# Attention scores by 64-row matmuls for all head pairs, masks by 64-row ones too, second buffers in the room of the kq tiles, and a new planned order

## The chip, the cores and the metric

The kernel runs on one core of one Trainium2 chip. A core has a TensorE (PE, matmuls, with its weight loads shown apart as PEld), a VectorE (DVE), a ScalarE (ACT), a GpSimd (POOL) and a SyncE (SP), whose queue here issues every DMA. The metric is the device time in microseconds (us) of one execution, and its median over several. A profile shows the span from the first to the last instruction, and the device time is a little longer than that.

## The reference, cut to what matters

Eight batches with eight heads of 576 tokens and 64 channels go through softmax attention with a block-causal mask (blocks of 64 tokens), and the result, 4608 tokens of 512 channels, through a feed-forward layer with 2048 hidden units and a rational activation.

```
scores = scale * np.matmul(q, k.transpose(0, 1, 3, 2))
mask = block_i >= block_j                      # blocks of 64 tokens
scores = np.where(mask, scores, -1000000000.0)
attn = softmax(scores)                         # over the last axis
x = (attn @ v), heads side by side             # 4608 x 512
h = x @ w_in
g = (a0 + a1 h + a2 h^2 + a3 h^3) / (1 + |b0||h| + |b1|h^2 + 1e-6)
out = g @ w_out
```

All of it is float32. The kernel keeps that accuracy with three products of split numbers: each operand is written as a high part in the fp32r format plus a low rest, and high*high, high*low and low*high are added.

## The kernel before, in words

**Attention.** Heads are worked in 32 pairs (`NP`), the two heads of a pair side by side in the 128 partitions. `load` fetches q, k and v of a pair. `prep` transposes q and k on TensorE (L410, three 96-row transposes into one PSUM bank), and ACT (L414) and DVE (L417) write the high and low halves into an `hl` tile: head 0 of the pair in partitions 0 to 63, head 1 in 64 to 127. `scores` works five stripes `t` of query rows, which see 64, 192, 320, 448 and 576 keys; the last stripe goes in two pieces of 288, and a piece is never narrower than 256 columns. Per piece and head come a maximum (DVE L521, L517), an exponential with its sum (ACT L525), a reciprocal and the scaling of the probabilities (POOL L532 to L545), their transposes (PE L566), a split of these into high (ACT L581) and low (DVE L583), and `pv`, the product with v (PE L604, 15 and 27 matmuls a pair), whose result is split (L617, L619) and stored to a scratch in HBM (L622). `vprep` splits v into the two `vpad` tiles (L453, L455).

**Two ways to score.** Pairs 0 and 1 (`nat`) score straight from the `hl` tiles: three matmuls with 64 rows for each head (L486), the two heads in turn, one in the upper and one in the lower half of the array, and the mask added by a small bf16 matmul with 32 rows for each head (L490). Pairs 2 to 31 score from `kq` tiles: eight DMAs a pair (L432) copy the `hl` halves so that one 128-row matmul makes high*high plus the mask (L509) and another makes the two mixed products (L510). The constant mask rows of the kq tiles are built at the start by POOL (L334 to L342) and copied by DVE (L362).

**Feed-forward.** `split_weights` splits the weights (`place`, 32 pieces: DVE L637 to L643, ACT L635, L647, L651, POOL L648, L652). In the first part of the program `ffn0` (PE L741, L760) works half of the hidden units for 256 tokens at a time between the attention work; when attention is done, its room takes the other half of the weights, and `ffn1` (PE L855, L858, L881) does the rest for 512 tokens at a time.

**The order.** Every operation is recorded with a cost, a priority and its dependences, and `Plan.order` plays a list schedule on these numbers: the order in which operations start there is the order of each engine's queue. Buffers come from `Pool`s, the eight PSUM banks from one pool with quotas (`QA` six for attention, `QH` and `QO` two each for ffn0). `gate` holds feed-forward work back until attention has come to a given pair.

The attention tiles exist once (`QR`, `VR`, `HL`, `P`, `XS`, `vpad`), the kq tiles twice:

```
    QR = tiles(att, 1, [LP, 2 * NL, D], F32, "qr")
    HL = [tiles(att, 1, [128, 2, S], F32R, f"hl{i}") for i in range(2)]
    P = [tiles(att, 1, [128, 2, NK[t]], F32, f"p{t}") for t in range(5)]
    kqt = [[att.tile([128, 4, S], F32R, name=f"kq{'ab'[i]}{'ab'[j]}") for j in range(2)] for i in range(2)]
```

Of the kernel before, what the change touches and what calls it, by code (L numbers as in the profile page):

```python
# [60 lines left out]
class Op:  # L61
    __slots__ = ("eng", "c", "d", "fn", "pri", "gives", "deps", "outs", "bufs", "n", "ready", "at", "end", "seq")


PORT = 220.0
LATENCY = {"PE": 250, "ACT": 40,
           "DVE": 40.0, "POOL": 150, "SP": 60.0, "-": 0.0}


class Plan:  # L70
# [5 lines left out]
    def op(self, eng, cd, fn, rd=(), wr=(), pri=0.0, after=(), port=False, gives=()):  # L76
        o = Op()
        o.gives = gives
        o.eng, o.c, o.d, o.fn, o.pri, o.seq = eng, cd[0] + PORT * port, cd[1] + PORT * port, fn, pri, len(self.ops)
# [14 lines left out]
        if eng in ("ACT", "DVE") and any(b.quota for b in bufs):  # L94
            o.pri -= 15
# [4 lines left out]
    def order(self):  # L100
# [14 lines left out]
        left = len(self.ops)  # L115

# [14 lines left out]
        while left:  # L131
            best = None
            for e in LATENCY:
# [4 lines left out]
                for p, s, o in sorted(able[e])[:24]:  # L138
# [93 lines left out]
def attn_ffn_kernel(  # L232
# [37 lines left out]
    X.free = []  # L270
# [30 lines left out]
    XS = tiles(att, 1, [128, 2, 320], F32R, "xs")  # L301
# [3 lines left out]
    vpad = [att.tile([128, 128 + 4 * 192], F32R, name=f"vp{x}") for x in "hl"]  # L305
# [3 lines left out]
    op("SP", (500, 100), lambda: nc.sync.dma_start(out=coef[:, 0:4], in_=ca.partition_broadcast(128)), wr=["ca"], pri=20)  # L309
    op("SP", (500, 100), lambda: nc.sync.dma_start(out=coef[:, 4:6], in_=cb.partition_broadcast(128)), wr=["cb"], pri=20)  # L310
# [14 lines left out]
    p0 = P[0].tiles[0]  # L325
# [75 lines left out]
    def prep(p, s, which):  # L401
# [18 lines left out]
        if p < NATP:  # L420
            return
# [528 lines left out]
```

## Time and profile before

| | |
|---|---|
| device time, median of 3 runs | 1282.99 us (1279.13 to 1284.53) |
| device time of the profiled execution | 1278.76 us |
| its span | 1276.6 us |
| PE busy | 1230.6 us, 96% |
| DVE, ACT, POOL busy | 942.3, 891.4, 848.5 us (74, 70, 66%) |
| DMA moved | 195.12 MB, mean 153 GB/s |
| 0 to 160 us: PE, DVE busy, mean PE clock | 133.28, 125.51 us, 0.93 |
| 160 to 800 us: the same | 628.53, 495.90 us, 1.00 |
| 800 us to the end: the same | 468.79, 320.88 us, 1.00 |

The first stage is attention with the weight split, the second attention between `ffn0`, the third `ffn1`. The ends of matmuls in the trace are modelled and overlap the next ones, so what a matmul costs is read from start to start. The granted clock has two levels, 1.0 (2.4 GHz) and 0.5 (1.2 GHz); the column of a window is their mean.

### The profile page before, as it was taken

Reading aid. Unit: us, or ns where it says so; the run is one execution under the profiler, and the core shown is the slowest. Engines: PE = TensorE matmul, PEld = TensorE weight load, DVE = VectorE, ACT = ScalarE, POOL = GpSimd, SP = SyncE. Lnnn points to the kernel's source line nnn. Section 1 sums busy time; section 2 is a strip of 40 time slices with the busy share of each in tenths; the row PEclk is TensorE's granted clock in tenths of the full one; section 3 lists DMA queues with packets and bytes.
Section 4 is the critical chain, followed back from the end, with each engine's and each line's share of the span. In section 5 each row is a group of like instructions: output and inputs, shape, how many; then the busy total and the mean of one; then the engine's idle time right before and its main releaser. Section 6 shows DMA issues by size and latency. Waiting matters only on the chain.

```text
span 1276.6 us, 23262 instructions
## 1 busy us (share of the span) xinstructions
PE 1230.6 (96%) x7560; PEld 1088.4 (85%) x7560; DVE 942.3 (74%) x1916; ACT 891.4 (70%) x2230; POOL 848.5 (66%) x1218
## 2 busy tenths in 40 slices
PE   7879999999999999999999999999999999999997
PEld 5669799899998999999988999888888888888885
DVE  7867887778787777778876876666676777677664
ACT  6778787778877788787787886555655555555554
POOL 6757876767767767676767776566665666665564
PEclk8989999999999999999999999999999999999999
DMA  5888876678777857786696741911142233224110
GB/s 147 217 235 213 221 191 174 179 191 210 192 194 185 225 162 200 180 212 187 165 236 181 196 133 63 379 47 41 59 132 67 89 109 118 81 66 132 34 33 33
DMA packets 222615, 195.12 MB, mean 153 GB/s; under 512 B 129312, under 2 KB 183584, under 8 KB 222496
## 3 DMA queue, kind: packets, MB, share of 16 engines
q1 hardware_dynamic: 222496, 193.65, 55.5%
q8 instruction: 60, 0.98, 0.3%
q14 instruction: 59, 0.48, 0.1%
HBM read 95.95 MB, written 44.56 MB: 110 GB/s over the span
## 4 chain that ended last, share of the span: by engine, by line
PE 68%; DVE 7%; DMA 7%; ACT 7%; POOL 6%; issue 3%; SPq 1%; POOLq 0%; ACTq 0%; DVEq 0%
PE psd L855 4%; PE psf L855 4%; PE psb L881 4%; PE psh L881 4%; PE pse L881 3%; PE psg L881 3%; PE psf L604 3%; DMA osa<-in_moe_w_in_dram 3%; PE psc L881 2%; PE psa L881 2%; PE psa L855 2%; PE psc L855 2%; PE psc L760 2%; PE psg L855 1%; PE psa L741 1%
## 5 line engine op out<-in xcount | busy, mean ns | idle before, releaser
L681 POOL TENSOR_SCALAR va<-ub,bab 128x512 f32<-128x512 f32 x60 | 46.8, 780 | 93.0 <-ACT ub L678 91.1
L681 POOL TENSOR_SCALAR vb<-ua,bab 128x512 f32<-128x512 f32 x57 | 44.2, 776 | 91.8 <-ACT ua L678 91.7
L703 POOL TENSOR_TENSOR glb<-sa,ghb 128x512 fp32r<-128x512 f32 x58 | 75.5, 1302 | 20.1 <-ACT ghb L702 17.7
L683 POOL TENSOR_TENSOR ub<-va,ub 128x512 f32<-128x512 f32 x60 | 77.9, 1299 | 4.6
L703 POOL TENSOR_TENSOR gla<-sb,gha 128x512 fp32r<-128x512 f32 x58 | 75.6, 1303 | 7.8 <-ACT gha L702 7.7
L455 POOL TENSOR_TENSOR vpl<-vra,vph 128x256 fp32r<-128x256 f32 (+1 forms) x128 | 67.8, 539 | 19.5 <-ACT vph L453 11.6
L683 POOL TENSOR_TENSOR ua<-vb,ua 128x512 f32<-128x512 f32 x57 | 74.0, 1298 | 4.6
L689 ACT ACTIVATE va<-ub,qcb 128x512 f32<-128x512 f32 x60 | 43.6, 727 | 46.0 <-POOL ub L683 45.8
L689 ACT ACTIVATE vb<-ua,qcb 128x512 f32<-128x512 f32 x57 | 41.3, 724 | 43.0 <-POOL ua L683 43.0
L702 ACT CAST ghb<-sa 128x512 fp32r<-128x512 f32 x58 | 36.1, 622 | 26.8 <-DVE sa L699 26.7
L702 ACT CAST gha<-sb 128x512 fp32r<-128x512 f32 x58 | 36.2, 624 | 11.1 <-DVE sb L699 10.9
L453 ACT CAST vph<-vra 128x256 fp32r<-128x256 f32 (+1 forms) x128 | 39.1, 324 | 1.8 <-POOL vph L323 0.4
L695 DVE SCALAR_TENSOR_TENSOR ub<-ub,psf 128x512 f32<-128x512 f32 x23 | 15.8, 686 | 25.5 <-ACT psf L693 25.4
L695 DVE SCALAR_TENSOR_TENSOR ub<-ub,psd 128x512 f32<-128x512 f32 x21 | 14.4, 687 | 26.5 <-ACT psd L693 26.3
L741 PE MATMUL psa<-x,wiha 128*128 128x256 f32 x176 | 33.2, 288 | 0.5 <-DVE sb L699 0.4
L741 PE MATMUL psf<-x,wiha 128*128 128x256 f32 x176 | 32.8, 285 | 0.5 <-DMA x<-xscr 0.5
L678 ACT ACTIVATE ua<-psf 128x512 f32<-128x512 f32 x25 | 15.0, 598 | 25.3 <-PE psf L855 21.1
L678 ACT ACTIVATE ua<-psd 128x512 f32<-128x512 f32 x24 | 14.3, 598 | 21.7 <-PE psd L855 19.4
L703 POOL TENSOR_TENSOR glb<-sb,ghb 128x512 fp32r<-128x512 f32 x14 | 18.1, 1296 | 16.1 <-ACT ghb L702 16.1
L741 PEld LDWEIGHTS psa<-x,wiha 128*128 128x128 f32 x176 | 27.3, 191 | 1.1 <-DVE sb L699 0.6
L741 PEld LDWEIGHTS psf<-x,wiha 128*128 128x128 f32 x176 | 27.5, 191 | 0.7 <-DMA x<-xscr 0.7
L741 PE MATMUL psb<-x,wiha 128*128 128x256 f32 x144 | 27.0, 286 | 0.0
(1662 smaller groups left out, 5599.0 us busy)
## 6 DMA issues: line engine op xcount, KB each, us to landing
xscr<-xsa SPq DMA_DIRECT2D x32, 320.0 KB, 2.9
x<-xscr SPq DMA_DIRECT2D x40, 256.0 KB, 4.5
qra<-in_q_dram SPq DMA_DIRECT2D x64, 144.0 KB, 3.7
qra<-in_k_dram SPq DMA_DIRECT2D x60, 144.0 KB, 2.9
vra<-in_v_dram SPq DMA_DIRECT2D x64, 128.0 KB, 2.5
xscr<-xsa SPq DMA_DIRECT2D x32, 256.0 KB, 3.7
ppa<-pscr SPq DMA_DIRECT2D x15, 512.0 KB, 4.0
osa<-in_moe_w_in_dram SPq DMA_DIRECT2D x10, 512.0 KB, 5.2
```

Source lines behind the costliest of these rows:

```text
L453: aop("ACT", (0.833 * n + 110, 0.833 * n + 200), lambda vh=vh, src=src: nc.scalar.copy(out=vh, in_=src()), rd=rd, wr=[("v", i, 0)], pri=pr ...
L455: aop("POOL", pool(n, True), lambda vh=vh, vl=vl, src=src: nc.gpsimd.tensor_tensor(out=vl, in0=src(), in1=vh.bitcast(F32), op=ALU.subtract ...
L604: nc.tensor.matmul(bank.t[:, s0:w], lhsT=vblock(vv, x), rhs=pp, start=(x == 0 and i == 0), stop=(x == nb - 1 and i == 2))
L681: op("POOL", pool(512, False, 2), lambda: nc.gpsimd.tensor_scalar(out=vt.t, in0=ut.t, scalar1=b1, scalar2=b0, op0=ALU.mult, op1=ALU.add), ...
L683: op("POOL", pool(512, True), lambda: nc.gpsimd.tensor_tensor(out=ut.t, in0=vt.t, in1=ut.t, op=ALU.mult), rd=[vt], wr=[ut], pri=pri)
L689: op("ACT", act(512, False, 1), lambda: nc.scalar.activation(out=vt.t, in_=ut.t, func=AF.Ln, bias=qcb), rd=[ut, "qcb"], wr=[vt], pri=pri)
L695: op("DVE", dve(512), lambda: nc.vector.scalar_tensor_tensor(out=ut.t, in0=ut.t, scalar=QC, in1=r0.t, op0=ALU.add, op1=ALU.mult), rd=rk, w ...
L702: op("ACT", act(512, False), lambda: nc.scalar.copy(out=gh.t, in_=st.t), rd=[st], wr=[gh], pri=pri)
L703: op("POOL", pool(512, True), lambda: nc.gpsimd.tensor_tensor(out=gl.t, in0=st.t, in1=gh.t.bitcast(F32), op=ALU.subtract), rd=[st, gh], wr ...
L741: nc.tensor.matmul(h.t[:, j * CT:(j + 1) * CT], lhsT=w[:, dc, fs], rhs=xb[dc // 2].t[:, dc % 2, hl, :], start=(dc == 0 and i == 0), stop=( ...
L855: nc.tensor.matmul(h.t, lhsT=w[:, dc, fs], rhs=x.t[:, dc, hl, :], start=(dc == 0 and i == 0), stop=(dc == 3 and i == 2))
L881: nc.tensor.matmul(o[m].t, lhsT=g.t[:, c0:c0 + 128], rhs=w[:, ff, :], start=(a and i == 0 and j == 0), stop=(z and i == 2))
```

## The change

All 32 pairs score as pairs 0 and 1 did: six 64-row matmuls a piece, two heads in turn. The mask tiles `mq` and `mk` get a copy in the lower half and 64 rows, so the mask matmuls are 64-row too, one in each half of the array. The kq tiles, their DMAs and the large mask go. In their room stand second buffers of `QR`, `VR`, both `HL`, `P[3]`, `P[4]`, `XS` and the `vpad` pair; pair 1 no longer borrows the room of `x`. The planner's costs change: it knows 93 ns for a change of the array's mode, new costs for matmuls and POOL; priorities and the gate change (`ffn0` may run 8 instead of 12 units ahead of attention, and begins at 70 instead of 60), `pv` falls behind the next pair's scores. Where the plan shows a gap on PE before a fresh bank in its first 160 us, up to 16 transposes of the identity are put into that bank ahead of its first use.

```
+MODE = 93.0
+WARM_UNTIL, WARM_SHARE, WARM_MOST = 160e3, 0.7, 16
...
+            if e == "PE" and o.rt != rt:
+                rt = o.rt
+                o.c += MODE
+                o.d += MODE
...
-    QR = tiles(att, 1, [LP, 2 * NL, D], F32, "qr")
+    QR = tiles(att, 2, [LP, 2 * NL, D], F32, "qr")
+    VR = tiles(att, 2, [128, 9, D], F32, "vr")
+    HL = [tiles(att, 2, [128, 2, S], F32R, f"hl{i}") for i in range(2)]
+    P = [tiles(att, (1, 1, 1, 2, 2)[t], [128, 2, NK[t]], F32, f"p{t}") for t in range(5)]
...
-    kqt = [[att.tile([128, 4, S], F32R, name=f"kq{'ab'[i]}{'ab'[j]}") for j in range(2)] for i in range(2)]
...
+    mq = cpool.tile([128, 128], BF16, name="mq")
+    mk = cpool.tile([128, 64], BF16, name="mk")
...
+            def sc(i=i, c0=c0, w=w, ww=ww):
+                for a, (x, y) in enumerate(((0, 0), (0, 1), (1, 0))):
+                    for j in range(2):
+                        r = slice(64 * j, 64 * j + 64)
+                        nc.tensor.matmul(bks2[j][i].t[:, :ww], lhsT=qt.t[r, x, qs], rhs=kt.t[r, y, c0:c0 + ww],
+                                         start=(a == 0), stop=(a == 2))
+                    if a == 0 and t and c0 + w == n:
                         for j in range(2):
                             r = slice(64 * j, 64 * j + 64)
+                            nc.tensor.matmul(bks2[j][i].t[:, w - 64:w], lhsT=mq[r], rhs=mk[r], start=False, stop=False)
...
-    E0, E1 = 60, 340
+    E0, E1 = 70, 345
...
     for o in todo:
+        if o.eng == "PE" and o.fresh and o.at < WARM_UNTIL:
+            for _ in range(min(int(o.gap * WARM_SHARE / 109), WARM_MOST)):
+                nc.tensor.transpose(o.fresh.t[:, :128], ident, ident)
         o.fn()
```

Between attention and `ffn0` on PE, in the kernel before: the rows of two heads' scores from the kq tiles (`kqaa`, `kqab`; L509 and L510) stand between the product with v (L604) and the second feed-forward matmuls (L760).

```order
L604 MATMUL psa<-pt2h,vpl 128x256
L509 MATMUL psh<-kqab 128x320
L510 MATMUL psh<-kqab 128x320
L509 MATMUL psg<-kqaa 128x448
L510 MATMUL psg<-kqaa 128x448
L760 MATMUL psc<-woha,gla 128x512
```

The same kind of place now, with the 64-row score matmuls (L448, from the tiles `hl1a` and `hl0a`), the mask (L453) and the first feed-forward matmuls (L690):

```order
L515 MATMUL psc<-ident,p4b 128x128 x3
L448 MATMUL pse<-hl1a,hl0a 128x256
L448 MATMUL psd<-hl1a,hl0a 128x256
L453 LDWEIGHTS mq
L453 MATMUL pse<-mk,mq 128x64
L453 LDWEIGHTS mq
L453 MATMUL psd<-mk,mq 128x64
L448 MATMUL pse<-hl1a,hl0a 128x256
L448 MATMUL psd<-hl1a,hl0a 128x256
L448 MATMUL pse<-hl1a,hl0a 128x256
L448 MATMUL psd<-hl1a,hl0a 128x256
L690 MATMUL psb<-x,wiha 128x256 x2
```

Two heads are now always scored together, and before and behind each such run of 64-row rows stands a 128-row row. In the whole program there are 147 runs, so 294 changes between 64 and 128 rows (78 of them up to the last L553 of pair 7), where the kernel before has 14.

At the head of PE's queue before, transposes of the raw q and k (`qra`, `osa`) and then the first scores:

```order
L410 MATMUL psa<-ident,qra 128x96 x3
L410 MATMUL psb<-ident,qra 128x96 x3
L410 MATMUL psc<-ident,osa 128x96 x3
L410 MATMUL psd<-ident,osa 128x96 x3
L486 MATMUL pse<-hl1a,hl0a 128x256
```

Now, with the transposes of the identity (L869):

```order
L869 MATMUL psa<-ident 128x128 x16
L395 MATMUL psa<-ident,qra 128x96 x3
L395 MATMUL psb<-ident,qra 128x96 x3
L869 MATMUL psc<-ident 128x128 x5
L395 MATMUL psc<-ident,osa 128x96 x3
L395 MATMUL psd<-ident,osa 128x96 x3
L869 MATMUL psf<-ident 128x128 x9
L448 MATMUL pse<-hl1a,hl0a 128x256
```

There are 181 of them in all, each in a bank that no real product has filled yet, and all before the 1,340th of some 8,300 matmuls.

In SP's queue before, a stretch with the copies into the kq tiles (L432), the load of k (L389, into the one tile `qra`) and a piece of weights (L633):

```order
L389 DMA qra<-in_q_dram 96x6x64 x2
L633 DMA osa<-in_moe_w_in_dram 128x2x512
L633 DMA osb<-in_moe_w_in_dram 128x2x512
L389 DMA qra<-in_k_dram 96x6x64 x2
L432 DMA kqaa<-hl0a 64x2x576
L432 DMA kqab<-hl0a 64x2x576
L432 DMA kqaa<-hl0a 64x576
L432 DMA kqab<-hl0a 64x576
L633 DMA osa<-in_moe_w_out_dram 128x1024
```

Now, with two raw tiles (`qra`, `qrb`) and no copies:

```order
L374 DMA qra<-in_q_dram 96x6x64 x2
L582 DMA osb<-in_moe_w_in_dram 128x2x512
L374 DMA qrb<-in_k_dram 96x6x64 x2
L571 DMA xscr_77<-xsa 128x2x320
L582 DMA osa<-in_moe_w_out_dram 128x1024
L673 DMA x<-xscr_77 128x2x256
L582 DMA osb<-in_moe_w_out_dram 128x1024
L571 DMA xscr_77<-xsb 128x2x256
```

The queue is 240 DMAs shorter, and the loads of q and k of a pair no longer wait for each other's tile.

## Rows read from the trace of the kernel before

**Rows 1.** The page: the span, PE's busy time, PE's, the clock's and the DMA engines' line of the 40 slices, the main DMA queue, and the head of the chain that ended last.

```profile
span 1276.6 us, 23262 instructions
PE 1230.6 (96%) x7560; PEld 1088.4 (85%) x7560; DVE 942.3 (74%) x1916; ACT 891.4 (70%) x2230; POOL 848.5 (66%) x1218
...
PE   7879999999999999999999999999999999999997
...
q1 hardware_dynamic: 222496, 193.65, 55.5%
...
PE 68%; DVE 7%; DMA 7%; ACT 7%; POOL 6%; issue 3%; SPq 1%; POOLq 0%; ACTq 0%; DVEq 0%
```

**Rows 2.** Busy time of each engine in stretches (from:to, length, then PE, PEld, DVE, ACT, POOL with counts, granted clock, DMA share, GB/s): the three stages, split at the end of pair 7's attention, and four slices of the first.

```profile
0.00:189.00 189.00, 162.16 (x1111) 141.35 (x1112) 150.35 (x372) 141.73 (x439) 135.36 (x242) 0.94 0.80 204
189.00:800.00 611.00, 599.65 (x4342) 559.01 (x4341) 471.06 (x1087) 479.85 (x1358) 428.33 (x721) 1.00 0.70 183
800.00:1276.60 476.60, 468.79 (x2111) 388.04 (x2110) 320.88 (x458) 269.85 (x434) 284.82 (x256) 1.00 0.29 94
...
20.00:40.00 20.00, 16.14 (x97) 12.65 (x97) 17.10 (x43) 15.04 (x49) 11.99 (x23) 0.74 0.62 157
60.00:80.00 20.00, 15.67 (x95) 13.51 (x94) 12.62 (x35) 13.20 (x44) 14.45 (x27) 0.83 0.97 254
80.00:100.00 20.00, 16.20 (x105) 14.77 (x104) 14.96 (x40) 15.27 (x51) 8.90 (x19) 0.84 0.89 225
120.00:140.00 20.00, 18.70 (x127) 15.96 (x126) 19.01 (x47) 16.77 (x50) 18.30 (x28) 1.00 0.78 193
```

**Rows 3.** The end of pair 7's attention: the ACT copy of its last product with v (timeline of ACT; start, length, operation).

```profile
188.10 0.38 ACT L617 CAST xsa<-psf 128x256 fp32r<-128x256 f32 x1 [0.34 <-PE psf L604]
```

**Rows 4.** A piece of the chain of waits at 90 to 103 us (start, length, what).

```profile
89.70 4.92 DMA qra<-in_k_dram
94.75 0.73 PE psb L410 x3
95.51 0.42 ACT hl1a L414
95.95 0.46 DVE hl1a L417
97.17 5.40 DMA kqba<-hl1a
```

**Rows 5.** The 128-row scores, timeline of PE around 291 us and at 480 us (start, length with its modelled end, operation, idle time before it).

```profile
291.41 0.37 PE L509 MATMUL psf<-kqab 128*128 128x448 f32 x1
291.61 0.37 PE L510 MATMUL psf<-kqab 128*128 128x448 f32 x1
291.82 0.30 PE L509 MATMUL psg<-kqaa 128*128 128x288 f32 x1
291.95 0.29 PE L510 MATMUL psg<-kqaa 128*128 128x288 f32 x1
...
479.90 0.28 PE L509 MATMUL pse<-kqaa 128*128 128x256 f32 x1
480.37 0.40 PE L760 MATMUL psg<-woha,glb 128*128 128x512 f32 x1
```

**Rows 6.** The 64-row scores of pair 1 at the full clock, with the mask, between transposes of both kinds: timeline of PE at 33 to 35 us.

```profile
33.04 0.41 PE L410 MATMUL pse<-ident,qra 96*128 96x96 f32 x3
33.38 0.39 PE L486 MATMUL psb<-x 64*128 64x288 f32 x1
...
33.62 0.29 PE L486 MATMUL psb<-x 64*128 64x288 f32 x1
...
33.75 0.29 PE L486 MATMUL psb<-x 64*128 64x288 f32 x1
...
33.88 0.29 PE L486 MATMUL psc<-x 64*128 64x288 f32 x1
...
34.51 0.29 PE L486 MATMUL psc<-x 64*128 64x288 f32 x1
...
34.73 0.33 PE L566 MATMUL psf<-ident,pkb 128*128 128x128 f32 x1
34.89 0.49 PE L566 MATMUL psf<-ident,p3a 128*128 128x128 f32 x3
35.22 0.49 PE L566 MATMUL psg<-ident,p3a 128*128 128x128 f32 x3
```

**Rows 7.** PE's waits between 160 and 800 us, the longest two and the shortest two of 18 (who, for whom: us in total, times, longest).

```profile
PE psc L509 <- DVE pt2l L583: 1.2, 3, 0.6
PE psf L410 <- DMA qra<-in_k_dram: 1.1, 1, 1.1
...
PE psc L566 <- POOL pkb L539: 0.2, 1, 0.2
PE psb L566 <- POOL p1a L545: 0.2, 1, 0.2
```

**Rows 8.** The start: PE's longest waits of the first 160 us, and the first of the eight DVE copies of the mask into the kq tiles.

```profile
PE psa L410 <- DMA qra<-in_q_dram: 4.4, 1, 4.4
PE pse L486 <- DVE hl1a L417: 2.5, 1, 2.5
...
L362 DVE CAST kqaa<-p4a x2: 800/942/1084, 2.6 to 5.6; 64x576 fp32r<-64x576 f32 x2
```

More of the change, by code (lines that the diff above doesn't have):

```diff
@@ L61 @@
 class Op:
-    __slots__ = ("eng", "c", "d", "fn", "pri", "gives", "deps", "outs", "bufs", "n", "ready", "at", "end", "seq")
+    __slots__ = ("eng", "c", "d", "fn", "pri", "gives", "deps", "outs", "bufs", "n", "ready", "at", "end", "seq", "gap", "fresh", "rt")
 PORT = 220.0
+MODE = 93.0
+MODE_PRI = 0.0
+WARM_UNTIL, WARM_SHARE, WARM_MOST = 160e3, 0.7, 16
 LATENCY = {"PE": 250, "ACT": 40,
-           "DVE": 40.0, "POOL": 150, "SP": 60.0, "-": 0.0}
+           "DVE": 40, "POOL": 90, "SP": 60.0, "-": 0.0}
 class Plan:
@@ L386, in load @@
         for which, src in ((0, q), (1, k)):
-            r = s["raw", which] = Buf(OS if which and p < NATP else QR)
+            r = s["raw", which] = Buf(OS if which and p < 2 else QR)
             for j in range(2):
@@ L401, in prep @@
     def prep(p, s, which):
-        pri = 10 * p - 10 + (1, 3)[which]
+        pri = 10 * p - 10 + (1, 7)[which]
         raw, sc = s["raw", which], (QSCALE, 1.0)[which]
-        hl = s["hl", which] = Buf((HLE if p < NATP and p % 2 else HL)[which])
+        hl = s["hl", which] = Buf(HL[which])
         for half in range(2):
-            bank = Buf(banks, QA, 1)
+            bank = Buf(banks, QA, 0)
             def tp(half=half, bank=bank):
@@ L499, in scores @@
+            c_ = 3 * (0.418 * ww + 5) + (60 if t and c0 + w == n else 0)
+            o_ = aop("PE", (c_, c_ + 180), sc, rd=qk + ["mask", (pt, "claim")] + [(x[0], "claim") for x in bks2], wr=[bks2[0][i], bks2[1][i]],
+                     pri=10 * p + 2 * t, after=before)
+            o_.rt = True
+            if not i:
+                gates[p * 10 + t * 2] = gates[p * 10 + t * 2 + 1] = o_
         for j in range(2):
             pri = 10 * p + 2 * t + j
-            kq = kqt[p % 2][j]
-            qs = slice(Q0[t], Q0[t] + 128)
@@ L503, in scores @@
-            kk = [("kq", p % 2, j, x) for x in ("q0", "q2", "k0", "k1")]
-            bks = bks2[j] if nat else [Buf(banks, QA, 1) for _ in pieces(t)]
-            for i, (c0, w) in enumerate(() if nat else pieces(t)):
-                ww = max(w, 256)
-                def sc(bank=bks[i], c0=c0, ww=ww, kq=kq):
-                    nc.tensor.matmul(bank.t[:, :ww], lhsT=kq[:, 0, qs], rhs=kq[:, 2, c0:c0 + ww], start=True, stop=False)
-                    nc.tensor.matmul(bank.t[:, :ww], lhsT=kq[:, 1, qs], rhs=kq[:, 3, c0:c0 + ww], start=False, stop=True)
-                o_ = aop("PE", mm(2, ww), sc, rd=kk, wr=[bks[i]], pri=pri, after=before + (kqmask[p % 2, j] if p < NATP + 2 else []))
-                if not i:
-                    gates[p * 10 + t * 2 + j] = o_
+            bks = bks2[j]
```

130 lines of the change are left out of this document (37 added, 93 removed).

## The prediction

> **What bounds the kernel now.** I read the page first: PE is busy for 96% of the span, and the chain that ended last is PE for 68% [rows 1]. A share over the whole span hides that stages differ, so the next view is busy time by stretches [rows 2]. The reader is to see three regimes. From 800 us on PE has nothing to wait for and nothing changes there. From 189 to 800 us PE is busy for 599.7 of 611 us and DVE for 471.1: PE bounds, and what is put into its queue ends up in the time. Up to 189 us, where pair 7's attention ends [rows 3], it is another matter: PE's slices show 7 and 8 at first [rows 1], the granted clock is 0.74 to 0.84 in three slices, the DMA engines stand at 0.97 and 0.89 [rows 2], and no engine is full: DVE has 150.4 of 189 us, 80%.
>
> Third, the chain of waits in that stage. Between 89.7 and 102.6 us it is a load of k (4.92 us), transposes, the split on ACT and DVE, and then a copy into a kq tile (5.40 us) [rows 4]. With one raw tile, one hl tile and a copy by DMA, a pair's scores come behind two DMA latencies and every buffer of the pair before. So the first stage is bound by this chain, not by an engine.
>
> **The change part by part.** I price the PE-bound stage first, then the first one, and add to the profiled execution's own time: span 1276.6 us, 2.2 us around it, 1278.8 us; the median of the runs is 4.2 us higher.
>
> *Scores.* Start to start, a 128-row score matmul takes 0.118 us at 256 columns (four from 479.90 to 480.37), 0.13 at 288 and 0.205 at 448 (two from 291.41 to 291.82) [rows 5]; for 320 I set 0.145 between them. A pair has stripes of 256, 256, 320, 448 and twice 288 columns, together 0.846 us, and four matmuls of each (two heads, two matmuls): 3.38 us. Of the 64-row matmuls the two heads' run side by side: one of each takes 0.13 us together at 288 columns (33.62 to 33.75 to 33.88) [rows 6]. Three such steps make 2.54 us. Saved: 0.85 us a pair.
>
> *Masks.* Today's 32-row mask adds much: from 33.88 to 34.51 stand two score steps and the mask, 0.63 us where two steps alone are 0.26, so 0.37 us [rows 6]. That includes two changes of rows, which a 64-row mask doesn't need. Its 64 columns alone would be 0.03 us (a quarter of 0.118). In between lies a weight load that the short mask can't cover: the first step behind a change took 0.24 instead of 0.13 us [rows 6], so a load that is not hidden costs 0.11. I take 0.11 us for each of four masks a pair, and keep 0.03 and 0.37 as ends.
>
> *Changes of rows.* Into 64 rows: three 96-column transposes begin at 33.04 and the score at 33.38. A 128-column transpose is 0.11 us (34.89 to 35.22 for three), a 96-column one in proportion 0.082, so 0.25 of the 0.34 us is work and 0.09 a gap; then the open load of 0.11: 0.20 us. Back to 128 rows: 34.51 to 34.73 is 0.22 for a step of 0.13, a gap of 0.09, and the first transpose takes 0.16 instead of 0.11: 0.14 us [rows 6]. In 105 of the 147 runs what follows is no transpose; the load of such a matmul may cost 0.11 in place of 0.05, so 0.20 is the upper end there. I take the row's 0.14: 0.34 us a run of 64-row matmuls. Behind pair 7 the changed order has 216 changes, 108 runs: 36.7 us.
>
> The Trainium skill (TensorEngine Tiling (Array Packing), Key Properties) says that changing the tiling mode, not just the tile, drains the TensorE, a rule against this change. The gap of 0.09 us on either side agrees [rows 6], but the rows add the open loads to it: by the drain alone the 108 runs would be 19.4 us and the time 17 us lower.
>
> So behind pair 7 PE gets 24 pairs x (-0.85 + 4 x 0.11) = -9.8 us, and +36.7: 27 us more, on the path that sets the end.
>
> *Waits of that stage.* PE's listed waits from 160 to 800 us run from 1.2 down to 0.2 us, 18 of them, 10.4 us together, for POOL, DVE and a k load [rows 7]. With 27 us more on PE its suppliers have more time, two raw tiles take the k load off, and some 3 us of loads that stand open behind transposes in the kq scores are now in the price of a change. I take -11 us (ends 0 and -13).
>
> *The first stage.* Gone are the eight DVE copies of the mask (two of each form, mean 0.94 us in the one shown, 6 us together), in front of which the first split had to queue: the first score waited 2.5 us for it [rows 8]. Gone are the kq copies, 240 DMAs and about 53 of 193.65 MB [rows 1] (6 x 147 KB a head), and with them one of the two latencies of the chain [rows 4]. The second raw, hl, P and v tiles let pair p+1 go through its transposes while pair p is in its exponentials. What is late next is an engine: DVE. Its work up to pair 7 is today's 150.4 us, less the 6 us of copies, less some 5 us of feed-forward that the new order puts behind pair 7, so 139. At DVE's best slice (19.01 of 20 us, 95% [rows 2]) this would end at 6 + 146 = 152 us; at today's 80% at 180. I take 88%: 164. PE's own sum up to there, by the same step prices over the changed order, is 132 us with 78 changes in it (13 us), so the changes are hidden beside DVE here; without that cover they cost those 13 us. The 181 transposes of the identity stand in gaps; if there is no gap they cost 0.11 us each, 20 us. From 188.5 to 164 is -24.5 us; 26 fewer L741 and 11 fewer L760 matmuls come before pair 7, which at 0.12 and 0.23 us ([rows 5] for the columns of the first, the second in proportion to 448) is 5.6 us paid later. Net -19 us; ends -31 and, with no gain, +6.
>
> *Sum.* 1278.8 + 27 - 11 - 19 = 1275.8; because the transposes can't all sit in true gaps I add 2 us: 1278 us. The saving of 0.85 us a pair is small beside the price of changing rows, and the first stage pays it back.
>
> **The rivals.**
>
> *Faster (1258).* The masks cost 0.03 us (-8) and the first stage goes at 95% (-12). For it: in the first stage the chain is DMA latency, and 120 to 140 us shows that DVE can be filled. Against: a stripe's steps pass from DVE to ACT to POOL to PE and back, and PE's waits for POOL are still there.
>
> *Slower (1297).* The runs of 64-row matmuls break PE's stream more than the rows of pair 1 show. Place: the 108 runs between feed-forward matmuls. Price: 0.20 us both ways (+6.5), a mask at 0.2 (+9), and as each run needs two PSUM banks at once, four in the last stripe, where the kq scores took one after the other, a third of the waits stay (+4). It decides from 0.35 us a run: there the 108 runs (38 us) take all that the waits, the first stage and the scores give (11 + 19 - 2 + 9.8). The row stands at 0.34, so this is near. Against: PE's queue behind pair 7 is full of feed-forward work that needs no bank of attention.
>
> *The clock stays down (1287).* The slices at 20, 60 and 80 us had 0.74, 0.83 and 0.84 of the clock [rows 2]: (0.26 + 0.17 + 0.16) x 20 = 12 us of clock lost, and PE then was at about 16 of 20 us. If the identity transposes don't prevent this, PE bounds part of the first stage and 9 us of its gain go. For it: transposes and scores alternate in these slices already. Against: the new order has no copies to wait for there.
> The Trainium skill (TensorE: Matmul & The Clock Gate, Part 4) says that transposes don't count as activity for the clock gate as matmuls do, by which these fillers would do nothing. No row here shows a stretch of transposes alone, so the trace neither agrees nor disagrees, and it stands as the reason for this rival's chance.
>
> **How the numbers follow.** Forecast 0.38, faster 0.27, slower 0.23, clock 0.12. What a measurement can tell from no change is about 0.5%, so 1276.6 to 1289.4 us counts as no change. The forecast's own range, 1269 to 1287, lies with 0.17 below, 0.18 within and 0.03 above; the faster rival gives 0.25 below; the slower one 0.21 above and 0.02 within; the clock rival 0.07 within and 0.07 above. That is 0.42 faster, 0.27 the same, 0.31 slower. The range reaches to both outer cases, 1256 to 1303: it leaves out the ends in which the first stage has no gain at all and full prices add up.
>
> **What the profile would show.** L448 pairs starting together and 0.13 us apart at 288 columns; a gap of 0.09 us and a first step of 0.24 at each run's head; the mask step 0.11 over the rest. Pair 7's last xs copy near 164 us, with DVE near 88% before it; a clock column at 1.0 from 20 us on; DMA bytes near 140 MB; between there and the start of the third stage PE's waits below a microsecond in all. The third stage keeps its length of about 476 us. The forecast is wrong if pair 7 ends after 180 us, if a run costs clearly more than 0.35 us, or if feed-forward matmuls wait for banks.

## The result and the profile after

The changed kernel takes 1289.12 us (median of 4 runs, 1288.12 to 1289.95), the kernel before 1282.30 us beside it. The ratio is 1.0057, with a 95% interval from 1.0039 to 1.0076: slower by 7 us, just over what can be told from no change. The forecast was 1278 us with faster as the likeliest, so its direction was wrong. The kernel before was timed again beside every run below, with medians from 1279.2 to 1282.3 us, so where two runs differ by 3 us or less only their ratios can be compared. One execution of before_filler took 5744 us and is left out of its ratio.

The page of the profiled execution (1289.69 us), its lines as in [rows 1]:

```profile
span 1287.9 us, 24324 instructions
PE 1267.4 (98%) x8341; PEld 1082.7 (84%) x8341; DVE 927.6 (72%) x1910; ACT 893.5 (69%) x2230; POOL 847.2 (66%) x1215
...
PE   8999999999999999999999999999999999999997
...
PEclk9999999999999999999999999999999999999999
...
q1 hardware_dynamic: 199456, 140.55, 36.5%
...
PE 81%; POOL 9%; DVE 3%; ACT 2%; DMA 2%; issue 2%; SPq 0%; POOLq 0%; ACTq 0%
```

The change did what it says: 53 MB of copies are gone and no slice of the clock column is below 9. But PE's share of the chain rose from 68% to 81%, and its busy time by 37 us. Where [rows 2] had PE at 162 of 189 us in the first stage, this is the busy time of each engine in stretches now (columns as there), split at the new end of pair 7's attention:

```profile
0.00:178.00 178.00, 169.78 (x1417) 144.59 (x1418) 150.04 (x374) 144.90 (x455) 138.09 (x253) 0.99 0.53 143
...
60.00:80.00 20.00, 19.86 (x181) 16.95 (x180) 18.89 (x49) 17.95 (x61) 16.41 (x31) 1.00 0.67 180
...
178.00:800.00 622.00, 618.28 (x4750) 541.40 (x4749) 461.45 (x1072) 474.93 (x1332) 417.40 (x701) 1.00 0.39 114
```

At 60 to 80 us, where PE had 15.67 and DVE 12.62 of 20 us, they now have 19.86 and 18.89, and ACT 17.95. The copy that ends pair 7, in ACT's timeline:

```profile
177.25 0.39 ACT L566 CAST xsb<-psf 128x256 fp32r<-128x256 f32 x1
```

That is 178 us, against 188.5 before [rows 3] and 164 in the forecast. PE's waits from 160 to 800 us, the first two and the last two of nine, 3.6 us together where [rows 7] had 10.4:

```profile
PE psa L395 <- DVE pt1l L532: 1.1, 2, 0.6
PE psh L690 <- DVE hl1b L402: 0.5, 1, 0.5
...
PE psd L515 <- POOL glb L652: 0.2, 1, 0.2
PE psh L515 <- POOL glb L652: 0.2, 1, 0.2
```

One run of 64-row matmuls between feed-forward (L690) and the product with v (L553), PE's timeline:

```profile
196.12 0.40 PE L690 MATMUL psf<-x,wiha 128*128 128x256 f32 x2
196.36 0.28 PE L690 MATMUL psf<-x,wila 128*128 128x256 f32 x1
196.57 0.39 PE L448 MATMUL psg<-hl1b,hl0b 64*128 64x288 f32 x1
196.57 0.40 PE L448 MATMUL psb<-hl1b,hl0b 64*128 64x288 f32 x1
196.81 0.20 PE L453 MATMUL psg<-mk,mq 64*128 64x64 bf16 x1
196.81 0.20 PE L453 MATMUL psb<-mk,mq 64*128 64x64 bf16 x1
196.85 0.38 PE L448 MATMUL psg<-hl1b,hl0b 64*128 64x288 f32 x1
...
197.06 0.29 PE L448 MATMUL psg<-hl1b,hl0b 64*128 64x288 f32 x1
197.07 0.29 PE L448 MATMUL psb<-hl1b,hl0b 64*128 64x288 f32 x1
197.20 0.29 PE L448 MATMUL pse<-hl1b,hl0b 64*128 64x288 f32 x1
...
197.47 0.29 PE L448 MATMUL pse<-hl1b,hl0b 64*128 64x288 f32 x1
...
197.69 0.38 PE L553 MATMUL psd<-pt2l,vph 128*128 128x256 f32 x1
197.92 0.28 PE L553 MATMUL psd<-pt2h,vph 128*128 128x256 f32 x1
198.03 0.28 PE L553 MATMUL psd<-pt2h,vpl 128*128 128x256 f32 x1
```

The weight loads (PEld) of the first score matmul, of one that follows another, and of the first two L553:

```profile
196.57 0.18 PEld L448 LDWEIGHTS psg<-hl1b,hl0b 64*128 64x128 f32 x1
...
197.34 0.18 PEld L448 LDWEIGHTS pse<-hl1b,hl0b 64*128 64x128 f32 x1
...
197.69 0.19 PEld L553 LDWEIGHTS psd<-pt2l,vph 128*128 128x128 f32 x1 [0.17 <-issue]
197.80 0.19 PEld L553 LDWEIGHTS psd<-pt2h,vph 128*128 128x128 f32 x1
```

Read the starts. The last L690 needs 0.12 us but the next row comes 0.21 behind it: a gap of 0.09. The first pair of score matmuls starts together and takes 0.24 instead of 0.13: its load starts with it at 196.57, where that of the matmul at 197.47 starts 0.13 ahead, at 197.34 (I call the first an open load). The mask moves the next start by 0.04, and the step behind it takes 0.21 instead of 0.13: 0.12 a mask. The last score step takes 0.22 (0.13 and a gap of 0.09), and the first L553, whose load is open too, 0.23 instead of 0.12.

I put every matmul's time from start to start into kinds: the plain step for its columns to the work, what is over to changes and masks, to waits, or, in stretches where the granted clock is 0.5 or no full clock is recorded yet, to the row "lower clock". That row therefore holds waits, masks and changes as well: the steps that take twice as long there cost 11 of its 19 us before, and 3 of 3 after. Stages end with pair 7, with the first `ffn1` matmul, and with the span:

```
us                           before                 after
stage                       1    2    3          1    2    3
feed-forward               30  301  466         24  304  468
P transposes, pv, q/k      73  209    0         74  207    0
scores                     28   80    0         23   58    0
masks and changes           3    0    0         19   53    0
identity transposes         0    0    0         20    0    0
lower clock                19    0    0          3    0    0
waits and the start        31   18    3         13    5    5
small gaps and the tail     5    8    4          3    5    4
together                  189  615  473        178  632  477
```

Against before, PE gains 26 us on scores, 16 in the stretches at the lower clock (8 of it by the clock itself), 29 on waits and the start and 6 on small gaps, and pays 68 for masks and changes and 20 for identity transposes: 11 us more, which is the spans' difference (sums before rounding).

### The profile page after: what moved, and what is told of

Read it like the earlier page. It is cut to its first block, busy times and chain, and to the rows that moved or that the text cites. A ratio compares the mean times of both kernels' runs of the same rounds, so it can differ in the third digit from the quotient of the medians.

```text
span 1287.9 us, 24324 instructions
## 1 busy us (share of the span) xinstructions
PE 1267.4 (98%) x8341; PEld 1082.7 (84%) x8341; DVE 927.6 (72%) x1910; ACT 893.5 (69%) x2230; POOL 847.2 (66%) x1215
## 4 chain that ended last, share of the span: by engine, by line
PE 81%; POOL 9%; DVE 3%; ACT 2%; DMA 2%; issue 2%; SPq 0%; POOLq 0%; ACTq 0%
PE psa L709 3%; PE psf L829 3%; PE psc L690 3%; PE psg L829 3%; PE psb L690 3%; PE psd L803 3%; PE psa L803 2%; PE psb L803 2%; PE pse L690 2%; PE psh L709 2%; PE psg L709 2%; PE psc L803 2%; PE pse L803 2%; PE psc L829 2%; PE psh L829 2%; PE psb L829 2%
## 5 line engine op out<-in xcount | busy, mean ns | idle before, releaser
L652 POOL TENSOR_TENSOR glb<-sb,ghb 128x512 fp32r<-128x512 f32 x60 | 78.0, 1299 | 89.4 <-ACT ghb L651 89.3
L652 POOL TENSOR_TENSOR gla<-sa,gha 128x512 fp32r<-128x512 f32 x59 | 76.9, 1304 | 47.8 <-ACT gha L651 47.2
L632 POOL TENSOR_TENSOR ub<-vb,ub 128x512 f32<-128x512 f32 x58 | 75.1, 1294 | 4.6
L638 ACT ACTIVATE vb<-ub,qcb 128x512 f32<-128x512 f32 x58 | 42.1, 726 | 51.7 <-POOL ub L632 51.6
L630 POOL TENSOR_SCALAR va<-ua,bab 128x512 f32<-128x512 f32 x57 | 44.5, 781 | 50.2 <-ACT ua L627 49.6
L632 POOL TENSOR_TENSOR ua<-va,ua 128x512 f32<-128x512 f32 x57 | 73.8, 1295 | 4.7
L630 POOL TENSOR_SCALAR vb<-ub,bab 128x512 f32<-128x512 f32 x58 | 46.1, 795 | 39.4 <-ACT ub L627 37.6
L651 ACT CAST ghb<-sb 128x512 fp32r<-128x512 f32 x60 | 37.2, 620 | 38.6 <-DVE sb L648 38.4
L638 ACT ACTIVATE va<-ua,qcb 128x512 f32<-128x512 f32 x57 | 41.2, 722 | 27.6 <-POOL ua L632 27.6
L651 ACT CAST gha<-sa 128x512 fp32r<-128x512 f32 x59 | 36.4, 617 | 24.5 <-DVE sa L648 16.5
L690 PE MATMUL psc<-x,wiha 128*128 128x256 f32 x208 | 39.6, 290 | 0.3 <-DVE pt0l L532 0.3
L690 PE MATMUL psb<-x,wiha 128*128 128x256 f32 x192 | 36.5, 290 | 0.0
L690 PEld LDWEIGHTS psc<-x,wiha 128*128 128x128 f32 x208 | 32.2, 190 | 2.2 <-DVE pt0l L532 0.6
L690 PE MATMUL pse<-x,wiha 128*128 128x256 f32 x176 | 33.7, 290 | 0.0
L690 PEld LDWEIGHTS psb<-x,wiha 128*128 128x128 f32 x192 | 29.8, 191 | 1.6 <-issue 0.4
L690 PE MATMUL psc<-x,wila 128*128 128x256 f32 x104 | 29.3, 282 | 0.0
L690 PEld LDWEIGHTS pse<-x,wiha 128*128 128x128 f32 x176 | 27.3, 191 | 0.7 <-issue 0.3
L690 PE MATMUL psb<-x,wila 128*128 128x256 f32 x96 | 27.1, 282 | 0.0
L448 PE MATMUL pse<-hl1a,hl0a 64*128 64x256 f32 (+3 forms) x105 | 26.7, 352 | 0.0
L448 PE MATMUL pse<-hl1b,hl0b 64*128 64x288 f32 (+3 forms) x108 | 26.4, 342 | 0.0
```

The lines of the kernel that those rows point to most:

```text
L448: nc.tensor.matmul(bks2[j][i].t[:, :ww], lhsT=qt.t[r, x, qs], rhs=kt.t[r, y, c0:c0 + ww], start=(a == 0), stop=(a == 2))
L630: op("POOL", pool(512, False, 2), lambda: nc.gpsimd.tensor_scalar(out=vt.t, in0=ut.t, scalar1=b1, scalar2=b0, op0=ALU.mult, op1=ALU.add), ...
L632: op("POOL", pool(512, True), lambda: nc.gpsimd.tensor_tensor(out=ut.t, in0=vt.t, in1=ut.t, op=ALU.mult), rd=[vt], wr=[ut], pri=pri)
L638: op("ACT", act(512, False, 1), lambda: nc.scalar.activation(out=vt.t, in_=ut.t, func=AF.Ln, bias=qcb), rd=[ut, "qcb"], wr=[vt], pri=pri)
L651: op("ACT", act(512, False), lambda: nc.scalar.copy(out=gh.t, in_=st.t), rd=[st], wr=[gh], pri=pri)
L652: op("POOL", pool(512, True), lambda: nc.gpsimd.tensor_tensor(out=gl.t, in0=st.t, in1=gh.t.bitcast(F32), op=ALU.subtract), rd=[st, gh], wr ...
```

## The experiments

**What a mask costs.** The mask matmuls are left out of the changed kernel.

```diff
-                    if a == 0 and t and c0 + w == n:
-                        for j in range(2):
-                            r = slice(64 * j, 64 * j + 64)
-                            nc.tensor.matmul(bks2[j][i].t[:, w - 64:w], lhsT=mq[r], rhs=mk[r], start=False, stop=False)
```

> The changed kernel without the mask matmuls (the scores of later keys stay in, so the softmax is not masked); the order is the same. From the trace a mask pair adds 0.039 us of its own and makes the next score step 0.202 instead of 0.119 us, 0.12 us together. Theory A (0.12 us, all on PE's path behind pair 7): 96 masks, 11.9 us, 1277 us. Theory B (the budget's whole row of 18.6 us behind pair 7 is the masks'): 1270 us. Theory C (hidden by waits of other engines): 1286 us or more.

Measured: 1277.67 us, ratio to before 0.9985 [0.9972, 0.9998], 11.5 us under the changed kernel. Theory A holds: 128 masks (four a pair) cost 0.09 us each in the time (0.07 by the two ratios), and 0.12 on PE. The forecast's 0.11 was close.

**What the changes of rows cost.** The same, with three 128-row matmuls a piece in place of six 64-row ones, so that no run changes rows (the order stays).

```diff
-                    for j in range(2):
-                        r = slice(64 * j, 64 * j + 64)
-                        nc.tensor.matmul(bks2[j][i].t[:, :ww], lhsT=qt.t[r, x, qs], rhs=kt.t[r, y, c0:c0 + ww],
...
+                    j = a % 2
+                    nc.tensor.matmul(bks2[j][i].t[:, :ww], lhsT=qt.t[:, x, qs], rhs=kt.t[:, y, c0:c0 + ww],
+                                     start=(a < 2), stop=(a > 0))
```

> As no_mask, and in place of the six 64-row matmuls of a piece stand three 128-row ones of the same columns, two into the first head's bank and one into the second's (both heads' channels are summed, so the scores are not the reference's). The steps are as many and as long, but TensorE never changes its rows. Theory A (a run of 64-row matmuls costs 0.39 us, 0.20 going in and 0.19 coming out, all on PE's path behind pair 7): 108 runs, 42 us less than no_mask, 1235 us, and less still by what the first stage gains. Theory B (the price of the prediction, 0.34): 37 us less, 1240 us. Theory C (half of it is hidden behind waits, which then appear): 20 us less, 1257 us.

Measured: 1252.54 us, 0.9784 [0.9763, 0.9805], 25 us under no_mask. PE's row of changes, 55.8 us in no_mask, is gone, but waits went from 22.9 to 48.1 us, and small gaps grew by some 11. Pair 7 ends at 176 instead of 177 us, so nearly all 25 us come behind it: in the first stage the changes were covered, as the forecast had it. PE's waits behind pair 7, the first six:

```profile
PE psa L395 <- DVE pt1l L527: 2.0, 2, 1.0
PE psb L510 <- DVE pt0l L527: 1.3, 1, 1.3
PE psc L510 <- POOL sa L596: 1.0, 1, 1.0
PE psh L685 <- ACT p3b L469: 0.9, 1, 0.9
PE psg L685 <- ACT p3a L469: 0.9, 1, 0.9
PE psb L510 <- POOL sb L596: 0.9, 1, 0.9
```

DVE, POOL and ACT come late once PE has less to do. Theory C was nearer: of what PE is spared, about half arrives in the time.

**Fewer changes.** The planner is told a higher price for a change (200 ns) and given a priority for matmuls of the same rows; 115 runs of 64-row matmuls instead of 147.

```diff
-MODE = 93.0
-MODE_PRI = 0.0
+MODE = 200.0
+MODE_PRI = 2.0
```

> The changed kernel with two numbers of its planner changed: a change of rows is priced at 200 instead of 93 ns, and PE's choice prefers by 2 units of priority what keeps its rows. The order then has 115 runs of 64-row matmuls instead of 147, with 191 identity transposes instead of 181. Theory A (each run is 0.39 us on PE's path): 32 runs, 12.5 us less, 1277 us, about the kernel before or a little under it. Theory B (longer runs hold more banks at once and hold up the chain of a pair, so that waits take what the runs give): 1285 to 1292 us.

Measured: 1293.44 us, 1.0103 [1.0084, 1.0121]. Masks and changes fell from 72 to 60 us and the waits rose by 11; pair 5 ends at 136 instead of 121 us. Theory B, a little above its range: what the changes save comes back as waits.

**The identity transposes.** First without them in the changed kernel (`WARM_MOST` 0), then 185 of them put into the plan's gaps of the kernel before.

> The changed kernel with the 181 transposes of the identity left out and nothing else; the order is the same. In its trace the first stage (to pair 7's last product with v at 178 us) holds 19.7 us of these transposes, and PE waits there only some 11 us. Theory A (they stand in PE's way, because PE has become the bound of that stage): pair 7 ends 8 to 16 us earlier and the time falls to 1273 to 1281 us. Theory B (DVE, busy for 95% at 60 to 100 us, is the bound and they only fill the gaps): waits take their place, 1287 to 1291 us. Theory C (they hold the clock up, as was meant): stretches at half clock come back, which cost the kernel before 19 us, and the time rises to 1295 to 1305 us.

Measured: 1290.02 us, 1.0076 [1.0057, 1.0095], the same as with them, and pair 7 at 178 us again. The row of the lower clock is 13.6 instead of 3.3 us (10 and 3 by the clock itself) and waits are 24 instead of 13 in the first stage, together about the 20 us of transposes. The time is Theory B's, but half of the room goes to Theory C's lower clock.

```diff
...
+        if o.eng == "PE" and o.fresh and o.at < 160e3:
+            for _ in range(min(int(o.gap * 0.7 / 109), 16)):
+                nc.tensor.transpose(o.fresh.t[:, :128], ident, ident)
```

> The kernel before with the identity transposes put into the gaps of its own plan (185 of them), and nothing else. Its trace shows 19 us lost to the half clock in the first 145 us, but PE waits there for another 23 us. Theory A (the first stage is bound by loads, copies and DVE, so a faster PE only waits more): 1277 to 1283 us. Theory B (the clock was a cost by itself): 10 to 15 us less, 1265 to 1270 us. Theory C (the fillers stand in the way of real work): 1286 us or more.

Measured: 1274.05 us, 0.9942 [0.9925, 0.9958]: faster than both kernels, and the fastest here that leaves nothing out. Time by stretches, the second slice of 20 us and the fifth:

```profile
20.00:40.00 20.00, 17.76 (x123) 14.84 (x122) 16.00 (x42) 14.54 (x48) 11.44 (x21) 0.83 0.59 151
...
80.00:100.00 20.00, 16.39 (x124) 15.78 (x123) 14.39 (x38) 14.18 (x46) 8.28 (x18) 0.91 0.97 240
```

The clock is 0.83 and 0.91 where [rows 2] had 0.74 and 0.84, and the row of the lower clock falls from 19.3 to 7.3 us (11 to 6 by the clock itself). Pair 7, though, ends at 187 instead of 188 us, and pair 31 at 789 instead of 794: most of the gain appears behind the stage in which they stand. The time lies between Theories A and B, and why the gain is spread so is open.

**The second buffers.** All of them undone, with a new plan.

```diff
-    QR = tiles(att, 2, [LP, 2 * NL, D], F32, "qr")
+    QR = tiles(att, 1, [LP, 2 * NL, D], F32, "qr")
...
```

> The changed kernel with every second buffer undone (q, k and v raw tiles, hl, P, xs, vpad single as before), planned anew: 129 runs of 64-row matmuls, 327 identity transposes. Theory A (the second buffers make the first stage faster): a pair takes 20 us again there, pair 5 ends at 140 us or later, the time is 1300 us or more. Theory B (it is the kq copies that went): pair 5 ends at 121 to 126 us and the time is 1285 to 1293 us.

Measured: 1314.27 us, 1.0264 [1.0235, 1.0293]. Theory A: pair 5 ends at 151 instead of 121 us, pair 7 at 200 instead of 178. PE is busy there for 190 of 200 us, with 327 identity transposes instead of 181 among it:

```profile
0.00:200.00 200.00, 189.77 (x1599) 163.32 (x1599) 149.54 (x378) 147.52 (x458) 132.27 (x249) 1.00 0.45 126
```

So this kernel is 25 us slower without the second buffers. How much of that is theirs alone is open: the order is new too, and the 146 further identity transposes, at 0.11 us some 16 us of PE, were not taken out.

**Only some pairs from the hl tiles.** In the kernel before, four pairs score so instead of two (`NATP` 4), with 64-row masks. The buffers are those of the kernel before, so pairs 1 and 3 have their hl tile in the room of `x`, as pair 1 had, and pairs 2 and 3, like 0 and 1, load their k into the staging tiles of the weights.

> The kernel before, in which pairs 2 and 3 too score from the hl tiles by 64-row matmuls, and the mask matmuls are 64-row; pairs 4 to 31 keep the kq tiles, and every buffer is single. It has 16 runs of 64-row matmuls instead of 7. Theory A (in the first stage the copies into the kq tiles are what a pair waits for): pair 3 ends at about 92 instead of 102 us and the time falls by 6 to 10 us, to 1270 to 1275 us. Theory B (the single buffers hold the stage up, not the copies): pair 3 ends at 100 to 104 us, the time 1278 to 1284 us.

Measured: 1307.33 us, 1.0211 [1.0185, 1.0238], slower than either theory has it, and Theory A falls. Pair 3 ends at 110 us (102 before), and PE stands at 12.73 of 20 us:

```profile
80.00:100.00 20.00, 12.73 (x68) 9.31 (x67) 15.88 (x41) 13.10 (x42) 13.49 (x25) 0.81 0.97 234
```

A missing second hl tile, which the expectation of second_hl_4 takes for the cause, can't be it: in the trace pair 3's scores read `x`, and pair 2's `hl1a` and `hl0a`. PE's longest wait between 76 and 110 us is 3.1 us for a load of q; which of the shared tiles costs most was not tried.

Three kernels carry this on from the kernel before with identity transposes and 64-row masks in pairs 0 and 1: one with measured costs of matmuls in the planner, and from that, two in which 4 or 6 pairs score from hl tiles, the odd ones' tile moved to the room of the second kq set.

```diff
-    c = max(cols / 2.4 * 1.04 + 9, 109)
+    c = max(0.418 * cols + 13, 109)
...
+    HLE = [Pool([kqt[1][i][:, 1::2, :]]) for i in range(2)]
...
-    NATP = 2
+    NATP = 4
```

> The kernel before with identity transposes in its plan's gaps (now 220), 64-row mask matmuls for pairs 0 and 1, and the measured step price of a matmul in the planner; kq tiles for pairs 2 to 31, all buffers single. Theory A (the fillers' gain of 7 us stays, the rest is noise): 1271 to 1277 us. Theory B (fillers beyond the earlier 185 delay real work): 1278 to 1284 us.

> As before_costs, and pairs 0 to 3 score from the hl tiles, the odd ones from second hl buffers that lie in the kq tiles of the second set, which no earlier pair uses; from pair 4 on the kq tiles serve. q's raw tile, v's raw tile and the rest stay single. 15 runs of 64-row matmuls. Theory A (what made the kernel with 64-row scores and single buffers slow was the one hl tile; with a second one the first stage goes at the changed kernel's pace of 16 us a pair, and behind it no row changes are paid): pair 3 ends at 88 to 92 us, the time 1260 to 1268 us. Theory B (the single raw and v tiles hold it too): pair 3 ends at 98 us or later, 1272 to 1285 us.

> As second_hl_4 with pairs 0 to 5 scored from the hl tiles; 25 runs of 64-row matmuls, all but a few in the first stage. Theory A: pair 5 ends at 121 to 128 us, the time 1260 to 1268 us. Theory B: pair 5 ends at 140 us or later, 1275 to 1290 us.

Measured: 1288.55 us (1.0052 [1.0035, 1.0070]), 1295.77 (1.0110 [1.0087, 1.0132]) and 1300.61 (1.0164 [1.0133, 1.0196]). For the last two Theory B holds for the pairs (pair 3 ends at 110 us in second_hl_4, pair 5 at 150 in second_hl_6), with times above its ranges: pair 2 comes at 72 and 67 us instead of 82, but pair 7 at 192 and 194. The first is above both of its theories, and it is the lesson: apart from the small masks and 35 more identity transposes (4 us at 0.11) only the planned order differs from before_filler, and it is 14 us slower, with waits of 53.2 instead of 38.1 us. Its longest waits behind 160 us are loads of k, which before_filler's list does not have:

```profile
PE psf L414 <- DMA qra<-in_k_dram: 1.8, 1, 1.8
PE psh L414 <- DMA qra<-in_k_dram: 1.0, 1, 1.0
```

**Another order of the changed kernel**: the old values of the gate.

```diff
-    def gate(pri, ahead=8):
+    def gate(pri, ahead=12):
...
-    E0, E1 = 70, 345
+    E0, E1 = 60, 340
```

> The changed kernel with the feed-forward of the first part beginning at 60 and running up to 12 ahead of attention, as in the kernel before, planned anew: 151 runs of 64-row matmuls, 183 fillers. In the changed kernel the fillers take 18 us of PE's first 121 us, time in which feed-forward matmuls could run. Theory A (the later start wastes PE's free time in the first stage): 4 to 8 us less, 1281 to 1285 us. Theory B (the first stage's other engines have no room for the feed-forward's elementwise work): the same within 3 us, 1286 to 1292 us.

Measured: 1295.65 us, 1.0112 [1.0093, 1.0130], 6.5 us slower, which neither theory had. Pair 7 ends at 184 us.

**What sets the first stage's pace.** First a lighter DVE: two of its three steps of a weight piece are gone, with a new plan.

```diff
-        op("DVE", dve(512, fast=True), lambda: nc.vector.tensor_scalar(out=i32(pt), ...
...
-        op("DVE", dve(512), lambda: nc.vector.scalar_tensor_tensor(out=i32(pt), ...
```

> The changed kernel without two of the three DVE operations of each of the 32 weight pieces (so the weights are not put together rightly); the order is planned anew. They take 0.64 and 0.89 us in the trace, 16 pieces in the first stage: 24 us of DVE's 150 us there, and 24 more behind it. Theory A (DVE is the bound of the first stage): pair 7 ends 12 to 18 us earlier, at 160 to 166 us, and the time is 1270 to 1277 us. Theory B (PE is the bound there, with its changes of rows and fillers): pair 7 ends at 174 us or later, 1285 to 1290 us.

Measured: 1290.09 us, 1.0072 [1.0044, 1.0099]: no gain, with DVE at 131.6 us of the first 178; pair 5 is later (127 us), pair 7 earlier (174). The new plan moved the order too, so three kernels keep the changed kernel's order word for word and make steps short instead: DVE's two, then ACT's first too, then without the identity transposes as well.

```diff
+TH = 32
...
-            out=i32(pt), in0=w0().bitcast(U32), scalar1=2.0 ** -29, ...
+            out=i32(pt)[:, :TH], in0=w0()[:, :TH].bitcast(U32), scalar1=2.0 ** -29, ...
...
```

> The changed kernel in its own order, with the first two of DVE's three steps of a weight piece on 32 columns instead of 512 and the third reading the same words twice (the split weights are wrong). Of DVE's 150 us up to pair 7 some 18 us go (16 pieces, 0.59 + 0.86 us today, about 0.15 each left... 16 x 1.15 us). PE's own sum up to there, with the identity transposes, is 167 us. Theory A, DVE's load sets the first stage's pace: pair 7 ends at 165 to 169 us instead of 178, and the time is 1277 to 1281 us. Theory B, the passage of a pair's steps through all engines sets it: pair 7 at 174 to 179 us, 1285 to 1290 us.

> As thin_dve, and ACT's first step of a weight piece on 32 columns too (0.73 us each, 16 of them before pair 7, about 9 us off ACT's 145; the weights are wrong). Theory A: pair 7 at 165 to 168 us, held there by PE's own 167 us, 1276 to 1280 us. Theory B: pair 7 at 173 to 178 us, 1284 to 1290 us.

> As thin_both, without the identity transposes (18 us of PE before pair 7, against some 10 us of lower clock that come back). Theory A, DVE's and ACT's load set the pace and PE only the floor: pair 7 at 155 to 165 us, 1265 to 1277 us. Theory B, the passage of a pair sets it: pair 7 at 172 to 178 us, as in no_filler, 1283 to 1290 us.

Measured: 1282.54 us (1.0017 [1.0005, 1.0029]), 1282.10 (1.0021 [1.0012, 1.0031]) and 1279.47 (1.0000 [0.9990, 1.0010]), with pair 7 at 172, 170 and 169 us. The result lies between the theories: DVE's work up to pair 7 goes from 150 to 137 us and pair 7 comes 5.5 us earlier; ACT's goes from 142 to 136, for another 2; and 20 us of identity transposes less on PE bring another 2. The slice from 60 to 80 us of the first and then of the third of these kernels:

```profile
60.00:80.00 20.00, 20.00 (x188) 17.23 (x187) 17.65 (x51) 18.64 (x65) 17.12 (x33) 1.00 0.68 192
...
60.00:80.00 20.00, 19.30 (x164) 15.83 (x163) 18.43 (x51) 18.21 (x65) 16.91 (x32) 1.00 0.68 193
```

With DVE relieved, PE is full; with PE relieved too, PE, DVE and ACT stand at 19.30, 18.43 and 18.21 of 20 us. In this slice no single engine sets the pace: three stand close to full. Behind pair 6 it is PE alone (next section).

## Why the prediction was wrong

**The failed step is the first stage**: "PE's own sum up to there ... is 132 us" beside a DVE of 139 us at 88%, so 164 us. Both terms were too small. In the table PE's own work up to pair 7, without identity transposes, clock and waits, is 143 us (24 + 74 + 23 + 19 + 3). Redone over the order that ran, the forecast's own prices and 13 us of changes give 136 us up to pair 7's last L553, not 132; the rest is small gaps, dearer changes, and work on PE between that L553 at 175 us and the copy at 178. With the 6 us before PE's first matmul on data and the 7 to 10 us that the clock itself costs in thin_both_nf and no_filler, PE alone needs close to 160 us, which leaves hardly any room for a wait. DVE's work was 150 us, not 139: about 1 us less of feed-forward left the stage than I took off, all of pair 8's maxima stand ahead of pair 7's end where fewer than half did before (with the steps behind them 6 us), and the weight steps took 4 us more (below). At 150 of 178 us it reached 84%. So pair 7 came 10.5 us earlier instead of 24.5. This is 14 us, and the forecast missed the profiled execution by 12.

The loss has a place. Pair 6's last copy, now and before (ACT's timelines), and the stretch from there to pair 7's end, now and before:

```profile
142.59 0.36 ACT L566 CAST xsb<-psf 128x256 fp32r<-128x256 f32 x1
...
165.81 0.37 ACT L617 CAST xsa<-pse 128x256 fp32r<-128x256 f32 x1
```

```profile
143.00:178.00 35.00, 33.87 (x248) 28.05 (x245) 28.93 (x64) 27.35 (x78) 29.09 (x50) 1.00 0.28 74
...
166.00:188.50 22.50, 22.38 (x175) 21.42 (x174) 19.27 (x44) 19.20 (x54) 17.61 (x29) 1.00 0.64 167
```

Up to pair 6 the change is 23 us ahead, almost the 24.5 of the forecast; then pair 7 takes 35 us where it took 22. PE is full there in both, DVE is not. In the 35 us stand 15 us of feed-forward instead of 10, 4 us of masks and changes instead of none, and more of pair 8. In thin_both_nf, with DVE and ACT relieved and no identity transposes, this stretch is still 34 us. So the end of the stage is bound by PE's sum, which the forecast set beside DVE's pace and took for covered.

**Scores**: -0.85 us a pair forecast; 80.1 to 58.5 us over 24 pairs, -0.90. This was right.

**Masks and changes behind pair 7**: forecast 36.7 + 24 x 0.44 = 47 us, measured 53, which with masks at 0.12 is 0.38 us a run: over the 0.35 that the prediction named as a sign of being wrong. The way into 64 rows is 0.20 us as forecast. The way out is 0.14 only to transposes; to fp32r matmuls it is 0.20, the upper end named for them. The Trainium skill (TensorEngine Tiling (Array Packing), Key Properties) gives the drain; here a gap of 0.09 us stands at each change, and the open load behind it costs as much again.

**Waits**: -11 forecast; 17.5 to 5.5 us, -12. This was right, with the work of PE as their cover: no_mask_128 brought them back.

**The second stage** was forecast at +21.6 us (27 - 11 + 5.6) and came to +17: 6 more for changes, 4 less of small gaps, and half of the late feed-forward falls into the third stage.

**The third stage** was to keep its length and got 5 us longer: 2.7 us of that feed-forward, and 2 us of waits. PE's waits there, the first three (the first two stood there before too, the third is one of five new ones of that size):

```profile
PE psg L829 <- POOL glb L652: 1.5, 1, 1.5
PE psg L829 <- POOL gla L652: 1.4, 1, 1.4
PE psc L829 <- POOL glb L652: 0.2, 1, 0.2
```

**The rivals.** *Faster (1258)* fell with both its terms: a mask costs 0.12 us on PE, not 0.03, and DVE reached 84%, not 95%. *Slower (1297)* named the right price of the way out and the right side, but not the cause: masks were 0.12, waits did not stay. *The clock stays down* is refuted: the mean clock of the first stage is 0.99. What no rival had is the order itself: plans with nearly the same work differ by 6.5 us (after_e60) and, with small changes, by 14 us (before_costs), as much as the terms of the sum, and as much as the 7 us by which the changed kernel is slower. A verdict on a kernel that was planned anew (grouped, single, light_place and the hl kernels) carries this uncertainty; no_mask, no_mask_128, no_filler and the three thin kernels keep their order and don't. The forecast took waits as if they went with the buffers and with PE's load; they also go with which of many near plans is played.

## What to carry to other kernels

Add up the work of every engine for the stretch that is to shrink, the one that looks idle too: here PE's 143 us, with the start and the clock close to 160, left 164 us almost no room, whatever DVE did. Price the way into and out of a packing that halves the rows of a matmul against the length of its runs: here a change there and back costs 0.4 us, three score steps, and a pair's 18 steps came in four or five runs. And before a change is credited with a few microseconds, plan the kernel a second time with slightly different costs, to see how far the order alone moves the time.

## What was not expected

**Transposes raised the clock.** The Trainium skill (TensorE: Matmul & The Clock Gate, Part 4) says that transposes do not count for the clock gate as matmuls do. Here they did, if `nc.tensor.transpose` runs in the mode that the page means, which the trace's rows (MATMUL) do not tell. PE's timeline at the start of the changed kernel, with nothing but transposes, and the granted clock in a stretch before its fall and one behind it:

```profile
1.34 3.42 PE L869 MATMUL psa<-ident 128*128 128x128 f32 x16 [1.34 <-POOL ident masks.py:199]
6.30 0.44 PE L395 MATMUL psa<-ident,qra 96*128 96x96 f32 x3 [1.53 <-DMA qra<-in_q_dram]
```

```profile
4.40:7.70 3.30, 1.72 (x16) 1.31 (x16) 0.48 (x2) 0.92 (x3) 1.44 (x5) 1.00 1.08 199
7.80:11.10 3.30, 3.30 (x21) 2.97 (x21) 1.15 (x3) 1.94 (x6) 1.86 (x4) 0.50 1.01 218
```

The 16 transposes take 0.21 us each, the pace of the lower clock; at 4.4 us the full clock is granted, before any other matmul has run. PE stood idle for 1.5 us up to 6.3; the clock falls at 7.8 us, and rises for good at 11.2. Without the identity transposes the first full clock is recorded at 14.9 us (before) and 21.7 us (no_filler).

**The same DVE instruction, slower.** The second step of a weight piece, one form, in the first 178 us of the changed kernel (least, median and greatest ns):

```profile
L589 DVE SCALAR_TENSOR_TENSOR sa<-osa,sa x8: 680/774/1647, 22.4 to 135.7; 128x512 int32<-128x512 int32 x8
L589 DVE SCALAR_TENSOR_TENSOR sb<-osb,sb x7: 784/1120/1586, 28.9 to 149.7; 128x512 int32<-128x512 int32 x7
```

Its mean went from 793 ns before to 958; the third step, of the same form, stayed at 818. The trace points to POOL: of all 16 steps 14 begin well inside a POOL instruction, and each of these ends 0.54 to 0.55 us after that instruction's end; the one that begins beside none takes 0.68, and the one that begins 8 ns behind a POOL instruction's start 0.67. No run took POOL's work away to confirm it.
